# Five more half sums of a hidden layer moved into the attention of the first batch, and a constant made earlier

## The chip, the cores and the metric

One NeuronCore of one Trainium2 chip runs the whole program. The metric is the time on the device in microseconds (us); a kernel's figure is the median of its runs. "The profile" is one execution taken by the hardware profiler. PE is the TensorE matmul engine, PEld its weight loads, DVE is VectorE, ACT is ScalarE, POOL is GpSimd, SP issues transfers. Kernels are compared with runs of the kernel before on the same chip in the same rounds.

## The reference

Attention in which a query sees only the keys with the same six-bit hash, then a mixture of eight experts whose weights come from eight normalisation rounds.

```python
# q, k, v: (4 batches, 8 heads, 768, 64), proj: (64, 6)
mask = bucket(q @ proj > 0)[:, :, :, None] == bucket(k @ proj > 0)[:, :, None, :]
attn = softmax(where(mask, q @ k.T / 8, -1e9))
x    = (attn @ v), heads side by side            # (3072, 512)
P    = exp(x @ w_gate), 8 rounds of row and column normalisation
out  = sum over e of P[:, e] * (relu(x @ w1[e]) @ w2[e])   # 8 experts, 512 -> 1024 -> 512
```

## The kernel before

The attention is a software pipeline of 192 units, 24 for each half batch (four heads, six key tiles). While the attention of one batch runs, a "filler" does expert 0 on the batch before it. The hidden layer of expert 0 is a sum of four products (`do` 0 to 3, 128 features each), and the first two need only heads 0 to 3. So the first half of it can be taken while heads 4 to 7 are still at work: units 34 to 42 do so for the first token half of batch 0.

```python
def first_part(fo):                                    # a half sum
    hp = ops.tile([P, 512], F32, tag="o")              # PSUM, two buffers
    for do in range(2):
        pin(nc.tensor.matmul(hp[:, 0:HT], w1[:, do, fo*P:(fo+1)*P], xT[:, do, 0:HT], ...))
    pin(nc.vector.tensor_copy(part[:, fo, :], hp[:, 0:HT]))

# in the filler, for a piece whose half sum exists ("short piece"): two products, then one DVE add
#   hT = relu(hp + part);            yield 325      (its PE time in ns)
# else: four products, then relu on DVE;  yield 650
...
for u in range(len(units) + 1):
    ...  scores(u + 1) ...                             # two matmuls `st`, ACT exponential `pt`
    values(u - 1)                                      # six matmuls `num`; after a head: nv, rn, xn on DVE
    if kt == 3 and h % 2 == 0 and u > 5:
        turn(...)                                      # transposes xn on PE, copy to xT on DVE
    elif 34 <= u < 43:
        first_part(u - 34 - (u > 39))
    elif u >= 2 * per:                                 # per = 24
        owed += (total - (8*325 if b == 1 else ...)) / (2*per - 8)
        while owed > 0:                                # the filler's pace
            owed -= next(fill)
```

`pin` keeps an instruction behind the last one traced on its engine. The `ops` buffers are shared by half sums, hidden pieces, hash products (`pr`, from which DVE makes the hash bits `bt`), transposes and gate.

The softmax here doesn't subtract the row's maximum and nothing guards it: scores larger than these inputs give would overflow.

## Time and profile before

| | before |
|---|---|
| time, first three runs | 766.67 us (766.44 to 767.45) |
| span of the profiled execution | 765.1 us |
| busy share PE / DVE / ACT / POOL | 98% / 74% / 67% / 42% |
| units 24 to 47 (second half of batch 0) | about 33 to 55 us |
| units 48 to 95 (batch 1, with the filler of batch 0) | about 55 to 106 us |

In the profile's lines the columns are start, length, engine, source line, operation, output and inputs, shape, and in brackets how long the engine stood idle before it and what released it.

### The profile page before, as it was taken

To read this page: it belongs to the slowest core of one execution; us is meant where nothing else is said; L and a number is where in the kernel's file an instruction comes from. 1 tells how busy PE (TensorE), PEld (TensorE's weight loads), DVE (VectorE), ACT (ScalarE), POOL (GpSimd) and SP (SyncE) were. 2 spreads that over 40 slices of the span, in tenths; PEclk is the share of its full clock that TensorE was granted. 3 is DMA by queue.
4 is the path that set the end of the run, shared out by engine and by line. 5 is a ranking of instruction groups with operands and counts; after the bars stand their busy time and mean duration, and the time that the engine had idled before them with its cause. 6 is when DMAs were issued, how large, how long until landed. Compare 5 with 4: busy or idle time off the path is not lost.

```text
span 765.1 us, 16738 instructions
## 1 busy us (share of the span) xinstructions
PE 747.5 (98%) x6294; PEld 517.2 (68%) x6294; DVE 567.4 (74%) x1261; ACT 514.0 (67%) x1027; POOL 318.3 (42%) x327
## 2 busy tenths in 40 slices
PE   8999999999999999999999999999999999999997
PEld 3655566566654677777777777777777777777664
DVE  6787666667579777777777777777777777777774
ACT  6986786678655777766666666666666666666661
POOL 6766353449200433443344334433543344324222
PEclk9999999999999999999999999999999999999999
DMA  8779447841030464776477648754964496443335
GB/s 227 203 195 227 126 128 174 175 124 27 2 56 8 83 108 80 125 126 115 90 130 132 112 84 144 121 95 83 171 118 90 91 165 112 84 84 83 84 77 145
DMA packets 41569, 88.08 MB, mean 115 GB/s; under 512 B 7232, under 2 KB 21840, under 8 KB 41488
## 3 DMA queue, kind: packets, MB, share of 16 engines
q0 software_dynamic: 27168, 69.49, 46.9%
q1 hardware_dynamic: 13324, 16.48, 8.2%
q10 hardware_dynamic: 996, 1.05, 0.6%
q8 instruction: 49, 0.80, 0.5%
q14 instruction: 32, 0.26, 0.1%
HBM read 53.05 MB, written 7.08 MB: 79 GB/s over the span
## 4 chain that ended last, share of the span: by engine, by line
PE 84%; DVE 6%; ACT 6%; issue 1%; DMA 1%; SPq 0%; ACTq 0%; DVEq 0%
PE a L829 18%; PE a L250 18%; PE d L829 13%; PE y L250 9%; PE st L570 6%; PE d L250 4%; ACT pt L573 4%; PE hp L647 4%; PE yp L662 3%; PE num L586 3%; PE pr L406 1%; PE hp L325 1%; PE yp L309 1%; ACT acc L241 1%; DVE hT L838 1%
## 5 line engine op out<-in xcount | busy, mean ns | idle before, releaser
L838 DVE CUSTOM_DVE_ANT_0 hT<-d,u 128x384 f16<-128x384 f32 x336 | 185.5, 553 | 96.2 <-ACT u L834 94.7
L254 ACT ACTIVATE vt<-a,p 128x256 f32<-128x256 f32 x324 | 153.3, 473 | 148.7 <-PE a L250 148.3
L834 ACT COPY u<-a 128x384 f32<-128x384 f32 x336 | 160.8, 479 | 23.5 <-PE a L829 19.9
L573 ACT ACTIVATE pt<-st 128x768 f16<-128x768 f32 x192 | 147.1, 809 | 42.5 <-PE st L570 41.8
L289 POOL DMA_DIRECT2D acc<-vt x72 | 62.0, 861 | 267.1 <-ACT vt L254 114.0
L250 PEld LDWEIGHTS <-hT 128*128 128x128 f16 x1296 | 126.3, 97 | 50.4 <-DVE hT L838 0.9
L250 PE MATMUL a<-t,hs 128*128 128x256 f16 x972 | 145.8, 273 | 2.2 <-ACT vt L254 1.0
L250 PEld LDWEIGHTS <-hs 128*128 128x128 f16 x972 | 94.8, 98 | 38.5 <-issue 2.8
L829 PEld LDWEIGHTS <-t 128*128 128x128 f16 x896 | 87.7, 98 | 36.4 <-issue 0.6
L829 PE MATMUL d<-xd,t 128*128 128x384 f16 x448 | 109.4, 326 | 0.3 <-DVE hT L838 0.3
L829 PE MATMUL a<-xT,s 128*128 128x384 f16 x448 | 109.4, 326 | 0.2
L570 PE MATMUL st<-qs,ks 71*128 71x384 f16 x384 | 94.0, 325 | 3.6 <-ACT pt L573 2.4
L250 PE MATMUL y<-t,hT 128*128 128x256 f16 x648 | 97.1, 272 | 0.0
L258 DVE SCALAR_TENSOR_TENSOR acc<-y,p,acc 128x256 f32<-128x256 f32 x162 | 77.4, 478 | 11.4 <-PE y L250 11.4
L134 POOL TENSOR_TENSOR t<-t 128x1024 f16<-128x1024 f16 (+1 forms) x39 | 81.9, 2108 | 0.1
L586 PEld LDWEIGHTS <-pt 128*128 128x128 f16 x1152 | 60.5, 97 | 25.9 <-ACT pt L573 0.4
L829 PEld LDWEIGHTS <-s 128*128 128x128 f16 x672 | 65.5, 98 | 17.5 <-issue 2.5
L586 PE MATMUL num<-va,pt 128*128 128x65 f16 x1152 | 66.5, 193 | 0.3 <-ACT pt L573 0.3
L868 ACT ACTIVATE hT<-a 128x384 f16<-128x384 f32 x112 | 54.0, 482 | 1.8 <-PE a L829 1.7
L829 PE MATMUL a<-xd,s 128*128 128x384 f16 x224 | 54.3, 323 | 0.8 <-ACT u L834 0.8
L829 PE MATMUL d<-xT,t 128*128 128x384 f16 x224 | 54.7, 326 | 0.0
L829 PE MATMUL a<-xT,t 128*128 128x384 f16 x224 | 54.7, 326 | 0.0
(121 smaller groups left out, 948.7 us busy)
## 6 DMA issues: line engine op xcount, KB each, us to landing
acc<-vt POOLq DMA_DIRECT2D x72, 512.0 KB, 4.8
t<-in_moe_w_dram POOLq DMA_DIRECT2D x26, 512.0 KB, 8.5
v<-in_v_dram POOLq DMA_DIRECT2D x28, 192.0 KB, 5.7
out_dram<-acc SPq DMA_DIRECT2D x78, 64.0 KB
acc<-in_k_dram POOLq DMA_DIRECT2D x6, 768.0 KB, 7.1
acc<-in_q_dram POOLq DMA_DIRECT2D x6, 768.0 KB, 12.2
t<-in_moe_w_dram POOLq DMA_DIRECT2D x3, 1024.0 KB, 12.0
ks<-t SPq DMA_DIRECT2D x60, 48.0 KB
```

Of the source, the lines that this page charges most:

```text
L134: pin(nc.gpsimd.tensor_tensor(o[:, sl], x[:, sl], y[:, sl], op=op))
L250: pin(nc.tensor.matmul(dst, hq[hn][:, fo, :], wq[wn][:, fo, :], start=first and fo == 0, stop=fo == FH - 1, skip_group_check=True))
L254: pin(nc.scalar.activation(out=vt[:, k], in_=a, func=Act.Copy, scale=p))
L258: pin(nc.vector.scalar_tensor_tensor(out=dst, in0=src, scalar=p, in1=dst, op0=Alu.mult, op1=Alu.add))
L289: pin(nc.gpsimd.dma_start(out=acc[:, b, i], in_=vt, accum_op=Alu.add))
L570: pin(nc.tensor.matmul(st[:, i, 0:HT], d["k"][0:KR, h, kt * P:(kt + 1) * P], d["q"][0:KR, h, i * HT:(i + 1) * HT], start=True, stop=True))
L573: pin(nc.scalar.activation(out=pt, in_=st[:, :, 0:HT], func=Act.Exp, scale=scale))
L586: pin(nc.tensor.matmul(num[:, j * (D + 1):(j + 1) * (D + 1)], pf[:, j * P:(j + 1) * P], va[:, h, kt, :], start=(kt == 0 and j == 0), stop= ...
L829: pin(nc.tensor.matmul(bk, wq[wn][:, do, f * P:(f + 1) * P], xq[xn][:, do, :], start=first and do == 0, stop=do == 1, skip_group_check=True))
L834: pin(nc.scalar.copy(t, bk))
L838: pin(add(TENSOR_ADD_SAT, out=dst, in0=bk, in1=u, s0=3e38, s1=0.0))
L868: pin(nc.scalar.activation(out=hT[:, f, hi], in_=a, func=Act.Relu))
```

## The change

The intent: five pieces of the second token half shall also be short, their half sums made in units 43 to 47 where no half sum was. And two instructions at the start are pinned, so that the "bit offsets", a constant made by four small DVE instructions, come first in DVE's queue.

```diff
-    part = acc_flat[:, 6 * DD:12 * DD].rearrange("p (f t) -> p f t", f=FO)
+    parts_of = [acc_flat[:, x * DD:(x + 6) * DD].rearrange(...) for x in (6, 0)]
+    halved = [(0, fo) for fo in range(FO)] + [(1, fo) for fo in range(5)]
-    def first_part(fo):
+    def first_part(t, fo):
         ... token half t, to parts_of[t] ...
     (filler)
-                half = b == 0 and t == 0
+                half = b == 0 and (t, fo) in halved
     (start)
-    nc.vector.memset(pb1, 0.0)
-    nc.vector.tensor_copy(pb1[R:2 * R, :, 0:NB], proj4[R:2 * R])
+    pin(nc.vector.memset(pb1, 0.0))
+    pin(nc.vector.tensor_copy(pb1[R:2 * R, :, 0:NB], proj4[R:2 * R]))
     (loop)
-        elif 34 <= u < 43:
-            first_part(u - 34 - (u > 39))
+        elif 34 <= u < 48:
+            first_part(*halved[u - 34 - (u > 39)])
-            owed += (total - (8 * 325 if b == 1 ...
+            owed += (total - (len(halved) * 325 if b == 1 ...
```

More of the change, by code (lines that the diff above doesn't have):

```diff
@@ L624, in gate @@
                                  in_=lg[:, 0:J * E], func=Act.Exp))
-    part = acc_flat[:, 6 * DD:12 * DD].rearrange("p (f t) -> p f t", f=FO)
-    def first_part(fo):
+    parts_of = [acc_flat[:, x * DD:(x + 6) * DD].rearrange("p (f t) -> p f t", f=FO) for x in (6, 0)]
+    halved = [(0, fo) for fo in range(FO)] + [(1, fo) for fo in range(5)]
+    def first_part(t, fo):
         hp = ops.tile([P, 512], F32, tag="o", name="hp")
         for do in range(2):
-            pin(nc.tensor.matmul(hp[:, 0:HT], weights[0, 1][:, do, fo * P:(fo + 1) * P], xT[:, do, 0:HT],
+            pin(nc.tensor.matmul(hp[:, 0:HT], weights[0, 1][:, do, fo * P:(fo + 1) * P], xT[:, do, t * HT:(t + 1) * HT],
                                  start=(do == 0), stop=(do == 1)))
-        pin(nc.vector.tensor_copy(part[:, fo, :], hp[:, 0:HT]))
+        pin(nc.vector.tensor_copy(parts_of[t][:, fo, :], hp[:, 0:HT]))
     def filler(b, blocks):
@@ L650, in filler @@
                 if half:
-                    pin(nc.vector._custom_dve(TENSOR_ADD_SAT, out=hT[:, fo, 0:HT], in0=hp[:, 0:HT], in1=part[:, fo, :],
+                    pin(nc.vector._custom_dve(TENSOR_ADD_SAT, out=hT[:, fo, t * HT:(t + 1) * HT], in0=hp[:, 0:HT],
+                                              in1=parts_of[t][:, fo, :],
                                               s0=3e38, s1=0.0))
@@ L741 @@
                 owed = 0.0
-        elif 34 <= u < 43:
-            first_part(u - 34 - (u > 39))
+        elif 34 <= u < 48:
+            first_part(*halved[u - 34 - (u > 39)])
         elif u >= 2 * per:
-            owed += (total - (8 * 325 if b == 1 else 8 * 865 if b == 3 else 0)) / (2 * per - 8)
+            owed += (total - (len(halved) * 325 if b == 1 else 8 * 865 if b == 3 else 0)) / (2 * per - 8)
             while owed > 0:
```

## The prediction

Passages with hardware figures that no trace or run of this case shows are cut, and each cut is marked. The sum came to +1.9 - 0.3 - 1.63 - 0.1 = -0.1 us, so 766.5. What the terms rest on stands in the profile of the kernel before. A matmul of 384 columns takes 0.163 us: four of a hidden piece take 0.65 us in the chain (63.60). The copy of a half sum takes 557 ns (median of eight). A half sum waits until DVE has copied out the one before last: PE's stand of 0.35 us at 47.55. DVE took `nv`, `rn`, `xn` and the copy in the order of the program: the half sum that PE had finished at 51.40 was copied only at 52.61. A "bank" is one of the two `ops` buffers; that there can be no third was not shown.

> **What bounds the kernel now.** I read the page first, then the stretches that the change touches: the busy times by stretch, the chain of waits from 40 to 74 us, and the PE and VectorE (DVE) timelines there and in the first 15 us. The page says PE is busy 98% of the span, at full clock in every slice, so in most of the kernel only removed PE work or removed PE gaps shorten the time. The busy times by stretch (length, then PE, PEld, DVE, ACT, POOL) show where that fails:
>
> ```profile
> 52.00:56.00 4.00, 3.62 (x46) 2.41 (x45) 2.51 (x4) 4.00 (x6) 3.42 (x6) 1.00 0.19 56
> 56.00:63.00 7.00, 6.09 (x93) 4.41 (x91) 6.59 (x13) 5.68 (x9) 4.76 (x8) 1.00 0.51 162
> 63.00:106.00 43.00, 42.27 (x462) 25.70 (x461) 28.45 (x54) 30.27 (x39) 18.82 (x29) 1.00 0.64 160
> ```
>
> From 52 to 56 ACT is full and DVE has 1.5 us free; from 56 to 63 DVE is nearly full; from 63 to 106 PE is full. The attention runs in units (one head, one sixth of the keys): a unit is two `st` matmuls, one exponential `pt` on ACT, six `num` matmuls, and filler. Units 24 to 47 are the second half of the first batch. Units 34 to 42 (without 39, which transposes) each carry one half sum `hp` today, units 43 to 47 none; the change puts five more there. The chain in that place:
>
> ```profile
> 50.15 0.82 ACT pt L573
> 50.98 0.82 ACT pt L573
> 51.82 0.56 ACT pt L573
> ...
> 53.26 0.66 ACT pt L573
> ...
> 53.97 0.69 ACT pt L573
> ...
> 54.70 0.66 ACT pt L573
> ...
> 58.52 1.83 DVE acc L395 x2
> ```
>
> The starts are 0.83 us apart where units carry a half sum (50.15, 50.98) and 0.72 us apart where they do not (53.26 to 54.70: 1.44 for two). So a unit with a half sum is set by PE (0.33 for `st`, 0.18 for `num`, 0.33 for `hp`, as the chain merges them: 0.84) and one without by ACT. PE has only about 0.2 us free per unit there, less than a half sum needs.
>
> [...] the copies of half sums show 557 ns (median of eight), so I use 557. [...] the half sum after next waits until DVE has copied this one out. [...]
>
> **The change, part by part.**
>
> *Removed.* Five second-token-half hidden pieces lose two of four matmuls in the second batch's filler: 10 x 0.163 = 1.63 us of PE, in the PE-full stretch (63 to 106). All of it is on the path. Their rectifying DVE step becomes an add with saturation, 558 ns against 557 ns for the old form: nothing.
>
> *Added.* The same 10 matmuls and five DVE copies (5 x 0.557 = 2.8 us) go to units 43 to 47.
>
> PE side: five units grow from 0.72 to 0.84 us, +0.6 us. Then the two buffers. Lines of the PE timeline and the DVE timeline:
>
> ```profile
> 47.55 0.48 PE L631 MATMUL hp<-xT,t 128*128 128x384 f16 x2 [0.35 <-DVE acc L633]
> ...
> 50.91 0.49 PE L631 MATMUL hp<-xT,t 128*128 128x384 f16 x2
> ```
>
> ```profile
> 51.94 0.75 DVE L607 TENSOR_TENSOR xn<-nv,rn 128x384 f16<-128x384 f32 x1
> 52.61 0.55 DVE L633 COPY acc<-hp 128x384 f32<-128x384 f32 x1
> 53.08 0.96 DVE L395 STREAM_TRANSPOSE acc<-acc 128x768 f32<-128x768 f32 x1
> 55.53 0.56 DVE L602 TENSOR_TENSOR nv<-num,mean 128x390 f32<-128x390 f32 x1 [1.49 <-PE num L586]
> ...
> 58.05 0.56 DVE L614 COPY xT<-xp 128x768 f16<-128x768 f16 x1 [0.24 <-PE xp L613]
> ```
>
> At 47.55 PE stood 0.35 us because a head's normalisation (`nv`, `rn`, `xn`) stood ahead of a copy. The same will repeat: the last old half sum (50.91) is copied out only at 52.61 to 53.16, behind `xn`. The new one of unit 43 starts at about 51.75 in the other buffer; that of unit 44 is ready at 52.59 and has to wait until 53.2: +0.6 us. Together +1.2 us on PE by unit 48.
>
> DVE side: today the key transpose of the next group (53.08, unit 48's) runs ahead of PE in the idle gap. Behind five copies it can't: they follow their matmuls (about 53.1, 53.7, 54.5, 55.4, 56.2), the transpose runs from 56.8 to 57.7, and only then come `nv`, `rn` and `xn` (done at about 59.0 against 56.9), the second transpose (60.0), and `xT` (L614). From 58.05 on today's DVE is dense until it frees the second batch's first hidden piece at 62.56, and PE waits for it (62.60, 0.33 us). Everything there moves by about 1.9 us. As the check: 2.75 us of copies at their pitch, less 1.75 us of today's gaps (1.49 + 0.24), plus about 0.85 us of new gaps between copies, is 1.85. So the 1.2 is inside this: **+1.9 us** by 62.6.
>
> *Moved.* The filler's rate falls from (21780 - 2600)/40 = 479 to (21780 - 4225)/40 = 439 ns a unit. I stepped the code's balance: today it gives 2, 1, 2, 1, 2 half sums to units 54 to 58, which the timeline confirms; afterwards 1, 2, 1, 2, 1. The last line matters, because in unit 58 DVE makes hash bits from a bank of the same pair:
>
> ```profile
> 62.60 0.48 PE L647 MATMUL hp<-xT,t 128*128 128x384 f16 x2 [0.33 <-DVE hT L651]
> ...
> 68.14 0.50 PE L647 MATMUL hp<-xT,t 128*128 128x384 f16 x2 [0.66 <-DVE bt L417]
> ```
>
> With one half sum in unit 58, unit 59's `st` and `num` (0.52 us) go ahead of the waiting one, so 0.66 falls to about 0.15. Against that, two in unit 57 make the hash wait about 0.25 us for its bank. Net **-0.3 us**.
>
> *The start.* The bit offsets (L79 to L83) run late today, between transposes and the first bits:
>
> ```profile
> 9.84 0.11 DVE L79 TENSOR_SCALAR row_i<-row_i 128x1 int32<-128x1 int32 x1
> ...
> 10.76 0.11 DVE L81 CAST qoff<-row_i 128x1 f32<-128x1 int32 x1
> ```
>
> The table's memset and copy were not pinned, so the transposes, pinned behind them, did not stand behind the offsets. Pinning them puts the offsets into DVE's idle time before 6.3 us. DVE gains about 0.3 us (10.84 to 11.16), but PE is then on nine warm-up matmuls (11.74 to 13.79), and the chain passes through the offsets for only 0.07 us; the first exponential also waits for DVE's q bits until 13.86. I count **-0.1 us**.
>
> *Sum:* +1.9 - 0.3 - 1.63 - 0.1 = -0.1 us, so 766.5.
>
> **Rivals.** (a) The backlog is smaller than I stepped it: if PE does not stop for unit 44's bank and DVE has drained by 58, only the 0.6 us of PE remains: +0.6 - 1.63 - 0.1 = -1.1, so 765.5. For it: DVE has 1.75 us of gaps in the stretch, and 47.55 cost only 0.35. Against: 2.8 us do not fit into 1.75. (b) The backlog persists: DVE, not PE, sets the first hidden pieces after 62 as well, and the hash waits longer. Then +2.5 - 1.63 - 0.1 = +0.8, 767.4. Against: DVE is busy only 28.45 of 43 us afterwards and had 0.92 us idle just before its bits at 66.61. (c) The removed PE work was hidden: ACT takes over in the second batch. Units there cost PE 0.52 plus 0.44 of filler, 0.96 us, well above ACT's 0.72, so no; if it were so, the loss of 1.9 would stand alone, 768.5. (d) The weights arrive late and absorb the gain: no PE gap stands in the timeline between 68.14 and 106, so the second weight's landing is not near.
>
> **Range and chances.** Rivals (a) and (b) span 765.5 to 767.4, and the kernel's own three runs 766.44 to 767.45. I lean slightly below the sum, since of the two errors a smaller backlog seems likelier: 766.4, range 765.3 to 767.4. Two per cent is 15 us; all the work touched is under 5 us, so anything but "within 2%" would need a stage outside 43 to 106 us to change.
>
> **What would show it.** In the new profile: thirteen copies of half sums, all before about 57 us; a PE wait of about 0.6 us for a copy at the second new one; the key transpose after the copies, at about 56.8; `xn` ahead of the last turn at about 59 and a PE wait for it; the first add-saturate at about 64.0 instead of 62.0; 13 of those and 35 plain rectifiers; the wait behind the hash bits mostly gone; the ACT-bound end of the second batch (106.0 today) within 0.5 us of its place; and all later stages shifted alike. I am wrong if the first hidden piece moves by under 1.2 us (then faster, rival a) or over 2.5 (rival b), if the start gains more than 0.3 us, or if the stages after 110 us change their length.

## The result, and the profile after

The changed kernel takes 768.22 us (768.01 to 768.91, six runs) against 766.81 us (766.44 to 768.04, six runs): 1.4 us slower. The ratio is 1.0018, 95% interval 1.0005 to 1.0031. All ratios here are the mean time of one kernel's fast runs over that of the other's of the same rounds, so not quite the ratio of the medians. The predicted 766.4 us (765.3 to 767.4) was too low; the class, within 2%, was right.

Busy times by stretch of the kernel after, for the three stretches that the prediction shows (length, then PE, PEld, DVE, ACT, POOL, the granted clock, the DMA share, GB/s):

```profile
52.00:56.00 4.00, 3.51 (x42) 2.36 (x41) 3.27 (x8) 3.25 (x5) 3.61 (x7) 1.00 0.46 122
56.00:63.00 7.00, 6.14 (x97) 4.50 (x96) 6.62 (x12) 6.55 (x10) 3.41 (x6) 1.00 0.21 54
63.00:106.00 43.00, 40.89 (x447) 25.03 (x447) 29.29 (x56) 29.66 (x40) 21.28 (x33) 1.00 0.69 174
```

From 52 to 56 ACT is no longer full. From 63 to 106 PE is no longer full: 2.1 us free where 0.7 were. As the work has moved by about 2 us, the fairer view is from the normalisation of unit 54 to that of unit 96 (stretch B below), first before, then after:

```profile
60.70:106.90 46.20, 44.66 (x484) 27.24 (x484) 31.20 (x59) 32.18 (x43) 21.44 (x34) 1.00 0.65 168
62.99:108.74 45.75, 43.34 (x474) 26.53 (x474) 30.87 (x59) 32.04 (x43) 21.61 (x34) 1.00 0.66 168
```

PE executes the ten matmuls fewer (474 against 484) and is busy 1.32 us less, but it is idle 2.41 us in place of 1.54. (The profile models the ends of matmuls, so the 1.32 need not be the 1.63 of the prediction.)

The DVE timeline after, at the first hidden piece. What came early in an idle gap before (53.08) now stands behind the fifth copy:

```profile
56.83 0.56 DVE L634 COPY acc<-hp 128x384 f32<-128x384 f32 x1 [0.28 <-PE hp L632]
57.30 0.97 DVE L395 STREAM_TRANSPOSE acc<-acc 128x768 f32<-128x768 f32 x1
...
58.98 0.59 DVE L607 TENSOR_TENSOR xn<-nv,rn 128x384 f16<-128x384 f32 x1
...
60.39 0.52 DVE L614 COPY xT<-xp 128x768 f16<-128x768 f16 x1
...
64.30 1.68 DVE L652 CUSTOM_DVE_ANT_0 hT<-hp,acc 128x384 f16<-128x384 f32 x3
```

The first add-saturate starts at 64.30 in place of 62.00. The PE timeline after, its stands on DVE:

```profile
53.80 0.48 PE L632 MATMUL hp<-xT,t 128*128 128x384 f16 x2 [0.49 <-DVE acc L634]
...
64.90 0.48 PE L648 MATMUL hp<-xT,t 128*128 128x384 f16 x2 [0.49 <-DVE hT L652]
...
67.71 1.50 PE L406 MATMUL pr<-acc,pb 128*32 128x384 f32 x16 [0.32 <-DVE hT L652]
...
73.97 0.49 PE L648 MATMUL hp<-xT,t 128*128 128x384 f16 x2 [0.99 <-DVE hT L652]
```

The last is the largest and was not predicted. What stood before it, again on DVE:

```profile
70.78 1.12 DVE L652 CUSTOM_DVE_ANT_0 hT<-hp,acc 128x384 f16<-128x384 f32 x2
71.85 0.56 DVE L602 TENSOR_TENSOR nv<-num,mean 128x390 f32<-128x390 f32 x1
...
72.68 0.77 DVE L607 TENSOR_TENSOR xn<-nv,rn 128x384 f16<-128x384 f32 x1
73.37 1.68 DVE L652 CUSTOM_DVE_ANT_0 hT<-hp,acc 128x384 f16<-128x384 f32 x3
```

In unit 60 a head ends, so DVE does `nv`, `rn`, `xn`; behind them wait the adds of two short pieces that PE made in the same unit. Unit 61's piece needs the first one's buffer, and PE waits until 73.97. In the kernel before, unit 60 had one long piece, and unit 61 did not wait (PE timeline before):

```profile
70.15 0.81 PE L647 MATMUL hp<-xT,t 128*128 128x384 f16 x4
70.80 0.49 PE L570 MATMUL st<-qs,ks 71*128 71x384 f16 x2
```

**A ruler for all runs.** When the first transfers land differs by up to 0.8 us between executions (those of `q`, which the chain of waits goes through, at 8.91 us before and 9.72 us after), so spans are poor evidence here. Instead I take the starts of the normalisation `nv` at units 30, 54 and 96 from each profile's timeline. Stretch A (30 to 54) holds the half sums and everything up to where the filler begins. Stretch B (54 to 96) holds the second batch. Behind unit 96 the kernels' rests are equal: 658.2 us before, 658.4 after (658.1 to 658.5 in the profiles of the experiments below, only pins_only has 659.0).

Each figure is one execution, and A is the less steady one. after_ahead and after_tuned below run the same program through A, and differ by 0.44 us in it; kernel after and halves_only by 0.51. The profiles show where this comes from: the `xn` of unit 42, behind which the next copy stands, takes 0.56 to 1.23 us, and PE's wait for a bank in unit 44 grows with it (0.59 and 0.31 us in cost_again, 0.78 and 0.49 in the kernel after, 1.23 and 0.94 in halves_only). DVE timeline of halves_only, then of after_ahead:

```profile
52.18 1.23 DVE L607 TENSOR_TENSOR xn<-nv,rn 128x384 f16<-128x384 f32 x1
```

```profile
51.58 0.56 DVE L607 TENSOR_TENSOR xn<-nv,rn 128x384 f16<-128x384 f32 x1
```

In all 14 profiles the `xn` of unit 36 takes 0.56 us with no POOL work beside it, while that of unit 42 falls into POOL's work on the next values; that POOL's work makes it longer is not tested. B is 46.19 or 46.20 in the four profiles whose B has the program of before, but 45.75 and 45.52 in the kernel after and halves_only, so 0.2 us in it is not sure.

| kernel | A, us | B, us | A+B against before |
|---|---|---|---|
| before (39.86, 60.70, 106.90) | 20.84 | 46.20 | |
| after (40.49, 62.99, 108.74) | 22.50 | 45.75 | +1.21 |

So A lost 1.66 us, B won back only 0.45 of the 1.63 us of matmuls that left it (2.17 and 0.68 in halves_only, below).

### The profile page after: what moved, and what is told of

The parts are those of the page before. It is cut to its first block, busy times and chain, and to the rows that moved or that the text cites. A ratio compares the mean times of both kernels' runs of the same rounds, so it can differ in the third digit from the quotient of the medians.

```text
span 767.1 us, 16743 instructions
## 1 busy us (share of the span) xinstructions
PE 748.3 (98%) x6294; PEld 517.3 (67%) x6294; DVE 569.7 (74%) x1266; ACT 515.2 (67%) x1027; POOL 318.9 (42%) x327
## 4 chain that ended last, share of the span: by engine, by line
PE 84%; DVE 8%; ACT 5%; issue 1%; DMA 1%; SPq 0%; ACTq 0%; DVEq 0%
PE a L831 18%; PE a L250 18%; PE d L831 13%; PE y L250 9%; PE st L570 6%; PE d L250 4%; PE hp L648 3%; PE yp L664 3%; PE num L586 3%; ACT pt L573 3%; PE pr L406 1%; PE hp L325 1%; PE yp L309 1%; ACT acc L241 1%; DVE acc L395 1%
## 5 line engine op out<-in xcount | busy, mean ns | idle before, releaser
L586 PEld LDWEIGHTS <-pt 128*128 128x128 f16 x1152 | 60.5, 97 | 25.9 <-ACT pt L573 0.4
```

Source lines behind the costliest of these rows:

```text
L586: pin(nc.tensor.matmul(num[:, j * (D + 1):(j + 1) * (D + 1)], pf[:, j * P:(j + 1) * P], va[:, h, kt, :], start=(kt == 0 and j == 0), stop= ...
```

## The experiments

Eleven further kernels ran, one of them twice (cost_only, cost_again). The times (us) first; those of one group share a chip and the runs of before.

| kernel | median | before | ratio (95%) | A | B |
|---|---|---|---|---|---|
| pins_only | 767.02 | 767.28 | 0.9994 (0.9981 to 1.0007) | 20.64 | 46.19 |
| halves_only | 768.25 | 767.28 | 1.0017 (1.0002 to 1.0031) | 23.01 | 45.52 |
| cost_only | 770.01 | 767.28 | 1.0037 (1.0019 to 1.0054) | 25.93 | 46.19 |
| saving_only | 766.07 | 767.28 | 0.9992 (0.9978 to 1.0006) | 20.73 | 45.84 |
| after_paced | 766.63 | 766.43 | 0.9997 (0.9984 to 1.0011) | 22.43 | 44.52 |
| after_ahead | 767.30 | 766.43 | 1.0008 (0.9994 to 1.0022) | 21.72 | 45.53 |
| before_tuned | 765.28 | 766.43 | 0.9982 (0.9970 to 0.9995) | 20.45 | 45.43 |
| three_tuned | 765.58 | 766.43 | 0.9986 (0.9974 to 0.9999) | 21.43 | 45.40 |
| cost_again | 768.10 | 766.82 | 1.0029 (1.0006 to 1.0052) | 22.17 | 46.20 |
| after_tuned | 766.62 | 766.82 | 1.0003 (0.9988 to 1.0019) | 22.16 | 44.64 |
| before_tuned_pins | 767.05 | 766.82 | 1.0000 (0.9988 to 1.0012) | 20.45 | 46.11 |
| two_tuned | 766.12 | 766.82 | 0.9993 (0.9978 to 1.0009) | 20.87 | 45.38 |

### The pins or the half sums?

pins_only is the kernel before with the two `pin( )`; halves_only is the kernel after without them.

> The kernel before with only the two pins, so that the bit offsets are made first. Theory (the loss is all in the five half sums; the q transfer that landed 0.8 us later in the changed kernel's profile is chance): within 0.2 us of before. Rival (the new order at the start costs what the profile's first 15 us show): slower by 0.5 to 0.7 us.

> The changed kernel without the pins. Theory: slower than before by 1.3 us (1.73 lost by the first hidden piece, 0.46 got back in the second batch). Rival (start to blame): slower by 0.7 us only.

The pins alone are neither slower nor clearly faster (0.9994, the interval holds 1), and B is unchanged. The half sums alone give the loss: 1.0017, near the 1.0018 of the whole change (A is 0.5 us longer than in the kernel after, 0.45 us of it because the wait in unit 44 was 0.94 us in that execution; its `xn` of unit 42 was 0.45 us longer). The rival that blamed the start asked for 0.5 to 0.7 us from the pins, a ratio of 1.0007 to 1.0009; pins_only's interval ends at 1.0007. It falls by that, and by A+B of halves_only, 1.49 us above before without any pin. In the profile the pins did what was meant; DVE timeline of the kernel after:

```profile
1.21 0.15 DVE L79 TENSOR_SCALAR row_i<-row_i 128x1 int32<-128x1 int32 x1 [1.21 <-POOL row_i L78]
1.40 0.15 DVE L81 CAST qoff<-row_i 128x1 f32<-128x1 int32 x1
```

They stand at 1.2 us where they stood at 9.84 and 10.76. From the landing of `q` to the first score matmul it takes 4.66 us (9.72 to 14.38) in place of 4.72 (8.91 to 13.63), and to the first exponential 5.18 in place of 5.36.

### The cost alone

The half sums of units 43 to 47 are made, but not used:

```diff
-                half = b == 0 and (t, fo) in halved
+                half = b == 0 and t == 0
-            owed += (total - (len(halved) * 325 if b == 1 ...
+            owed += (total - (8 * 325 if b == 1 ...
```

> The five half sums are made in units 43 to 47 but not used; the second batch computes all four products as before (right result). Theory: +1.7 us against before, lost between 51 and 63 us (five units at 0.84 in place of 0.72, one wait of about 0.65 us for a bank, and the DVE behind by 1.7 us when the first hidden piece is due). Rival (the loss arises in the second batch, from the shorter pieces): +0.6 us or less.

The ratio was 1.0037 and A 25.9 us: more than expected, and the profile shows why, before any line that the edit touches. PE timeline, then the busy times from 48.6 to 52 us of cost_only, with the granted clock third from the end:

```profile
46.73 0.48 PE L570 MATMUL st<-qs,ks 71*128 71x384 f16 x2 [2.56 <-issue]
```

```profile
48.60:52.00 3.40, 3.40 (x22) 1.95 (x21) 2.25 (x6) 1.98 (x3) 1.16 (x2) 0.53 1.08 311
```

PE stood 2.56 us at unit 36, and less than 2 us after its end the clock fell to 0.53. It is a single event, and that the stand made the clock fall is not tested. What PE waited for the profile does not show; meanwhile SP took 5.24 us, against 2.41 before, to issue four transfers of key rows (those of the next group, by the program's order). So I ran the same kernel again.

> The same kernel as cost_only, whose profiled execution stood 2.56 us at 46.7 us and then ran about 3.5 us of matmuls at half speed, before anything that the change touches. Theory (that was chance): no such stand this time; the shift against the kernel before grows by 1.6 to 1.8 us between the start of unit 43 and the first hidden piece and stays there to 106 us. Rival (the unused half sums make it): the stand comes back.

The stand did not come back in the profile: A is 22.17 us, +1.33 against before and +1.53 against pins_only, B exactly 46.20. The time ratio is 1.0029, with one run of 772.82 us at a clock of 0.994 in it; the other three are 767.83 to 768.15, 1.0 to 1.3 us above the median of before. So the five half sums cost about 1.3 to 1.5 us in A by this one profile, a little less than expected, and nothing in B. One thing stays open: five of the ten runs of this kernel took 769.7 us or more, and none of the kernel before did (at most 769.09). The profiled stand came ahead of anything that the edit touches, but no profile shows the other slow runs.

### The saving alone

No half sums in units 43 to 47, but 13 short pieces (the last five add an old half sum; the result is wrong):

```diff
-        elif 34 <= u < 48:
+        elif 34 <= u < 43:
-                                              in1=parts_of[t][:, fo, :],
+                                              in1=parts_of[0][:, fo, :],
```

> Wrong result on purpose: no half sums in units 43 to 47, but thirteen short pieces in the second batch (the last five add an old half sum). Theory (short pieces need 0.56 us of DVE for 0.33 us of PE, so two of them behind a head's normalisation or the hash bits make PE wait whether or not DVE was late before): only 0.4 to 0.8 us faster than before, with PE waits of about 1.1 us more than before between 63 and 75 us. Rival (those waits are inherited from the backlog of the first batch): the whole 1.6 us faster, or more.

B is 45.84: 0.36 us saved of 1.63, without any backlog from batch 0 (A 20.73). The PE timeline of saving_only has two of the stands of the kernel after:

```profile
64.60 1.50 PE L406 MATMUL pr<-acc,pb 128*32 128x384 f32 x16 [0.33 <-DVE hT L652]
...
70.95 0.48 PE L648 MATMUL hp<-xT,t 128*128 128x384 f16 x2 [1.09 <-DVE hT L652]
```

So they are not inherited. The rival falls: short pieces make these waits by themselves. The times (0.9992, interval to 1.0006) are too coarse to decide it; B decides.

### Is it the amount of DVE work or its order? The pace

The filler counts a short piece as 500 ns, so units get one of them and never two:

```diff
-                    yield 325
+                    yield 500
-                      (len(halved) * 325 if b == 1 ...
+                      (13 * (650 - 500) if b == 1 ...
```

> The changed kernel, but the filler counts a short piece as 500 ns, not 325, so that units 54 to 67 get one short piece each and never two. Theory (PE's waits after 64 us come from two short pieces falling into one unit behind DVE work): the three waits there (0.32, 0.14 and 0.99 us in the changed kernel, 1.96 us of lost PE time in all) shrink to 0.6 us or less, and the kernel is about 1.3 us faster than the changed one, level with before (within 0.4 us). Rival (DVE simply has too much work there, however it is spread): waits of the same sum, no gain.

B falls to 44.52, 1.68 us less than before, as much as the 1.63 us of removed matmuls. But it is not all theirs: the pace shortens the B of the kernel before too, to 45.43 (before_tuned, below), and against that the removed matmuls bring 0.91 us. Of the waits for DVE in B two small ones are left (PE timeline of after_paced):

```profile
71.01 0.48 PE L648 MATMUL hp<-xT,t 128*128 128x384 f16 x2 [0.27 <-DVE hT L652]
...
76.59 0.81 PE L648 MATMUL hp<-xT,t 128*128 128x384 f16 x4 [0.40 <-DVE hT L652]
```

A is as in the kernel after (22.43). The time comes back to that of before (0.9997). DVE has the same work in B here as in the kernel after, and B is 1.23 us shorter, so much of the loss in B was the order of that work, not its amount. The 0.72 us still missing (1.63 less 0.91) is about what these two waits add up to, 0.67 us.

### The order in batch 0

Where a head ends (units 36 and 42), the half sum goes ahead of the normalisation:

```diff
+        if u in (36, 42):
+            first_part(*halved[u - 34 - (u > 39)])
         if u > 0:
             values(*units[u - 1], pts.pop(u - 1))
```

> The changed kernel, but in units 36 and 42 the half sum is issued ahead of the head's normalisation, so DVE copies it out first. Theory (the wait in unit 44 is the order of DVE's queue, and DVE is the bound from 57 to 64 us): the waits at the first sums after each normalisation (0.35 and 0.49 us) go, the first add-saturate comes 0.6 to 1.1 us earlier relative to the first half sum, and the waits after 64 us stay. Rival (banks too few whatever the order): waits move to the next half sum and nothing is gained.

The stands of 0.35 and 0.49 us at half sums are gone. A is 21.72, 0.78 us less than in the kernel after (0.22 us of it may be the shorter `xn`, 0.56 against 0.78); B stays bad (45.53, with PE waits of 0.33 and 0.78 us at 65.73 and 71.78). Expected were 0.6 to 1.1 us. 0.9 us of A's loss is left. That DVE and PE together have too little room for all five is my reading of it; no run isolates it.

### Both remedies, with zero, two, three and five further half sums

before_tuned is the kernel before with both remedies (a short piece counted as 620 ns); two_tuned, three_tuned and after_tuned have two, three and five further half sums (590, 560, 500 ns); before_tuned_pins adds the pins to before_tuned.

> The kernel before with both remedies (half sums of units 36 and 42 ahead of the normalisation, a short piece counted as 620 ns), without the change. Theory: the 0.35 us wait at unit 38 and the 0.66 us wait behind the hash bits go or shrink: 0.5 to 1.0 us faster than before. Rival: nothing, as such waits only move.

> The changed kernel with three more half sums in place of five, and both remedies (560 ns for a short piece). Theory: DVE's 1.75 us of gaps hold three copies (1.65 us), so the first hidden piece is late by only 0.4 us of PE work, and 0.98 us of PE work is saved: 1.0 to 1.5 us faster than before, and faster than the kernel before with both remedies by about 0.5 us. Rival (any copy there delays DVE by its own length): no faster than the kernel before with both remedies.

> The changed kernel with both remedies (ahead of the normalisation in units 36 and 42; a short piece counted as 500 ns). Theory (the two remedies act on separate waits, so they add): about 1.3 + 0.9 = 2.2 us faster than the changed kernel, 0.8 to 1.1 us faster than before. Rival (DVE's sum bounds the stretch): no more than the paced version gained.

> The changed kernel with two further half sums in place of five, and both remedies (590 ns for a short piece). Theory (two copies, 1.1 us, fit DVE's 1.75 us of gaps; 0.65 us of PE work saved for 0.25 us spent): 0.2 to 0.5 us faster than the kernel before with both remedies and the pins. Rival (DVE is what counts, so any further copy costs what it saves): equal within 0.2 us.

> The kernel before with both remedies and the two pins, without further half sums. Theory (pins are worth 0 to 0.3 us): 1.2 to 1.5 us faster than before, the fastest of all. Rival: as fast as without the pins, within noise.

before_tuned beats both kernels: 765.28 us, ratio 0.9982 (0.9970 to 0.9995), about 1.2 us, with none of the change's further half sums. The 0.66 us stand behind the hash bits and the 0.35 us stand at unit 38 are gone. That is a little more than the 0.5 to 1.0 us expected, on one chip and five runs.

Against it, further half sums cost in A 0.42 us (two), 0.98 (three) and 1.71 (five), for 0.65, 0.98 and 1.63 us of matmuls removed from B, of which B shows 0.05, 0.03 and 0.79 (the first two with a new wait in them, below). So even if B got all of it, three would only pay for themselves by these profiles. They are single ones: the `xn` of unit 42 took 0.84 us in three_tuned and 1.02 in after_tuned, with waits of 0.33 and 0.50 us behind it, against 0.60 and no such wait in two_tuned; a part of the 0.98 and the 1.71 is this. I had expected three copies to fit DVE's gaps at a cost of 0.4 us; the rival (no gain over before_tuned) is the one that held in the times. By the times, two_tuned (0.9993), three_tuned (0.9986) and after_tuned (1.0003) are all no faster than before_tuned (0.9982). after_tuned did not reach the 0.8 us expected of it: its profiled A is 22.16, though B (44.64) kept the gain of the pace. A is partly a chance: half sums waited 0.50 us for DVE at 53.68, behind the long `xn`, and after_ahead, the same program up to there, had 21.72 without that wait.

before_tuned_pins was to be the fastest and was not (1.0000). Its profile has a new wait, and three_tuned's too (two_tuned's one of 0.16 us); PE timeline of before_tuned_pins, then of three_tuned:

```profile
77.90 0.48 PE L570 MATMUL st<-qs,ks 71*128 71x384 f16 x2 [0.64 <-DMA ks<-ds]
```

```profile
79.10 0.48 PE L570 MATMUL st<-qs,ks 71*128 71x384 f16 x2 [0.60 <-DMA ks<-ds]
```

Here the scores of the next group wait for hash bits on their way through memory. Once the filler runs faster, this transfer is at the edge: before_tuned passed it without a wait, before_tuned_pins lost what it had won. Whether the pins push it over the edge or chance does, these runs do not settle.

## Why the prediction was wrong, step by step

- **Five units from 0.72 to 0.84 us, a wait in unit 44, DVE's backlog: +1.9 us.** Right in mechanism and nearly in size. The transpose moved behind the copies, `xn` ended at 59.57 in place of 56.92, the wait for a bank was 0.49 us, and the first add-saturate came 2.30 us later, 0.57 of which was there at 51.1 us already: 1.73 us. By the ruler A lost 1.66 us. The 0.84 us of a unit with a half sum held (half sums start at 54.64, 55.47, 56.31), though the chain's lines quoted for it name ACT, not PE.
- **Removed: 1.63 us, "All of it is on the path".** This is the step that failed. PE did execute ten matmuls fewer in B, but B shrank by 0.45 us (0.68 in halves_only). Its waits for DVE there add up to 1.95 us (0.49, 0.32, 0.15, 0.99) where they were 0.99 before (0.33, 0.66): 0.96 of the 1.18 us that did not arrive. I had read from PE's 42.27 of 43 us that a matmul removed there shortens the time. Here it did so only as far as DVE kept up piece by piece: a short piece takes 0.33 us of PE and 0.56 us of DVE.
- **Moved: "Net -0.3 us".** This failed with it. I stepped the filler's balance only to unit 58, because that was where the kernel before stood. Up to there it came out in kind: the wait behind the hash bits fell from 0.66 to 0.15 us (the `num` ahead of that piece ends at 70.65, the piece starts at 70.80), and the hash itself waited 0.32. But two short pieces next fall into unit 60, behind a head's normalisation, and cost 0.99 us at 73.97. The same stepping, two units further, would have found it. after_paced shows what the order of the pieces cost: 1.23 us between 45.75 and 44.52, of which the pace wins 0.77 us without further half sums too.
- **The start: -0.1 us.** Right in kind: 0.06 us to the first score matmul and 0.18 to the first exponential in the profile, nothing to be seen in the times.
- **Rivals.** (b), DVE setting the first hidden pieces and the hash waiting longer, named the right place and the right sign (767.4). I set it aside because DVE is busy only 28.45 of 43 us there: an average over 43 us, used against a queue in which the work comes in lumps. (b) too counted the 1.63 us as won, so its 767.4 fell short. (c) came nearest in number (768.5), by luck: ACT was busy only 29.66 of 43 us afterwards.
- **Sum.** -0.1 us was predicted. In B, 0.45 us was won in place of 1.63 + 0.3, which is 1.48 short; A cost 0.24 less than the 1.9. That makes +1.1 to +1.2, as the ruler shows (+1.21); the timed medians differ by 1.4, inside the scatter of single runs (about 1 us).
- **The tests named beforehand.** Thirteen copies (last at 56.83), 13 add-saturates and 35 plain rectifiers came as said. The ACT-bound end of the second batch was to stay within 0.5 us of its place and came at 108.03 (106.19 before, 0.63 us of the difference being there at unit 30 already). None of the signs named for being wrong came up: the first hidden piece moved by 1.73 to 2.30 us, between 1.2 and 2.5. They tested the cost; none of them tested that the saving arrives.

## What to carry to other kernels

Work that moved off a full engine was won here only as far as the engine that empties its buffers kept the faster pace in each short stretch (0.45 of 1.63 us in B, with 1.95 us of PE's waits for DVE); step the queue of that engine through all of the stretch, not only through the place that waits now. A pacing rule can count a piece by the engine that takes longest over it: here this one number was worth more (1.23 us in B of the kernel after, 0.77 in that of the kernel before) than five removed half pieces without it (0.45). Two rotating buffers were enough where a piece took PE longer than DVE (0.65 against 0.56 us, the long pieces of the kernel before), and PE stood 0.99 us when two pieces of 0.33 us came behind 1.5 us of other DVE work (kernel after, 73.97). And where a copy frees one of two buffers, issue it ahead of unrelated work on the same engine: in after_ahead the stands of 0.35 and 0.49 us went.
